# Linear attention with a two-layer network on one core: query features transposed by DMA, middle chunks in row halves

## The chip, the core and the metric

The kernel runs on one core of a Trainium2 chip. Its time is device microseconds of one execution. Five engines work at once, each through its own queue in order: TensorE (PE, with its weight loads as PEld), VectorE (DVE), ScalarE (ACT), GpSimd (POOL) and SyncE (SP), which issues all DMAs here. They wait for each other by semaphores.

## What is computed

For 8 batches x 8 heads, sequence 576, head size 64, 128 random features:

```python
def phi(x):                                   # x = q or k, scaled by 64 ** -0.25
    h = einsum('bhsd,md->bhsm', x, omega) - sum(x * x, -1) / 2
    return exp(h - max(h, -1)) / sqrt(m)
kv  = einsum('bhsm,bhsd->bhmd', phi(k), v)
num = einsum('bhsm,bhmd->bhsd', phi(q), kv)
den = einsum('bhsm,bhm->bhs', phi(q), sum(phi(k), 2))[..., None] + 1e-06
x   = (num / den)                             # to 4608 tokens x 512
h   = x @ w_in                                # 512 x 2048
out = (h * sigmoid(h)) @ w_out                # 2048 x 512
```

All of it is in fp32. The two large products of the network are done with operands cut into a high and a low part, three matmuls for one.

## The kernel before, in words

**Attention.** The 64 heads are taken as 32 pairs n = 0 to 31, four to a batch. A pair has 2 x 576 = 1152 rows, cut into nine chunks of 128; the fifth, the middle chunk (`MID`), has the last 64 rows of one head and the first 64 of the other. For the 24 pairs from the third batch on (`FOLD` holds the pairs of the first two), a pair's steps are these. Two projections (`project`, L477), one for k, one for q, make four chunks of each head; head size 64 fills only half the rows of the array, so that the two heads run in its two row halves at once. The middle chunks of k and q are two more products over the full height (`project_mids`, L495), on a tile with zeros in the unused half. Then maxima (`top`, `top_mids`), shifts, exponentials (`expo`, or `lower` and `expo_all`), the sums of k's features (`sums`, `zsum`), the denominators (`denom`), and q's features times their inverse (`normal`, on POOL, in three groups of three chunks). The features have rows along the partitions, and the last product needs them the other way. So each group of three chunks is transposed on TensorE into a PSUM bank (`turn`, L636) and copied to SBUF by ScalarE (`en_copy`, L640). The pair's last unit (`kv_numer`, "kvnum") multiplies them with kv, and makes kv of the next pair as well.

**The network.** Stages 1 and 2 (`stage1`, `stage2`), then blockwise products by Strassen's scheme in three levels (`deep`, `product`), all of them groups of three matmuls of 128x128 by 128x512 (`thrice`, L831). ScalarE and VectorE cut their operands into parts (L873, L877) and take the results out of PSUM. The attention units are let in between these products, and the products that need late tokens come late.

**The order.** Every step is a unit of a plan: engine, function, what it comes after, what tile of which ring it takes (`RINGS`) and what it frees. A written-out list (`RANK`) gives each unit its place; the units are issued in that order, so each engine's queue is in the order of ranks. `HOMES` says from which of three pools the units take their PSUM banks. `FILL` and `TRAIL` put extra matmuls on ones around named units, `warm` puts eight products on ones ahead of the first projection. The times in the plan's code are not used when the kernel runs.

Of the kernel before, what the change touches and what calls it, by code (L numbers as in the profile page):

```python
# [9 lines left out]
F32R = mybir.dt.float32r  # L10
U32 = mybir.dt.uint32
# [29 lines left out]
NORM_DVE = tuple(range(9, 12))  # L41
SQUARES = {}
# [5 lines left out]
FILL = {("turn", 3, 0): 4, ("turn", 3, 1): 1}  # L48
TRAIL = {("mid", 2, "q"): 9}
# [20 lines left out]
    "in": 4, "v": 2, "sq": 2, "hk": 2, "hq": 2,  # L70
    "mxk": 2, "mxq": 2, "nbk": 2, "nbq": 2, "mxm": 2, "nbm": 2, "t": 1, "es": 1, "kt": 1, "kw": 2,
    "en": 2, "den": 2, "rd": 2, "g0": 4, "g1": 4, "g2": 4, "g3": 4, "ts": 3, "w": 7, "ic": 2, "c": 3,
# [40 lines left out]
def turn_of(c):  # L113
# [8 lines left out]
    "mid": "full", "mids": "full", "z": "few",  # L122
# [17 lines left out]
class Plan:  # L140
# [225 lines left out]
def attention_mlp(ctx: ExitStack, tc: tile.TileContext, qX, kX, qS, kS, qT, kT, qn, kn, v, om_in, w_in, w_out, out):  # L366
# [52 lines left out]
    def load_raw(n, who):  # L419
# [5 lines left out]
        if n in FOLD:  # L425
            nc.sync.dma_start(both[:D, : 2 * S], (kS if who == "k" else qS)[b, k])
            return
        T["raw", n, who] = raw = both[:, : S + P]
        nc.sync.dma_start(raw, (kT if who == "k" else qT)[b - FOLDED, k])

    def load_nat(n, who):
# [1115 lines left out]
```

## Time and profile before

| | |
|---|---|
| median of 3 runs | 956.26 us (955.84 to 956.85) |
| profiled execution | span 954.4 us |
| TensorE busy | 942.7 us, 5740 matmul records |
| VectorE, ScalarE, POOL busy | 772.1, 619.8, 392.4 us |
| DMA | 237.87 MB, 73.0% of 16 engines' span |
| records of L831 (network) | 3120 |
| records of L636 (transposes of q's features) | 288 |

The page gives the span of the profiled execution; its whole time is not listed beside it, and the runs are 1.9 us longer than the span. Busy time of TensorE counts matmuls that overlap in its pipeline, so the starts of its records say more about pace than their lengths.

### The profile page before, as it was taken

The page shows a single profiled execution, that of the slowest core. Times are in us where ns is not written, and L with a number is a line of the kernel's source. Part 1 is how long each engine was busy: PE and PEld are TensorE (multiplying, and loading weights), DVE is VectorE, ACT ScalarE, POOL GpSimd, SP SyncE. Part 2 cuts the span into 40 slices and gives each one's busy share as a digit, 9 for nine tenths or more (in the row PEclk, how much of TensorE's full clock was granted, in tenths as well). Part 3 has the DMA queues.
Part 4 walks back from the last instruction along what each step waited for, and adds up shares of the span by engine and source line. Part 5 has one row for each costly group of instructions (what it writes and reads, how often), then busy time and mean ns, then how long its engine had stood idle before and what let it go on. Part 6 is the DMA issues. An engine that isn't in the chain of part 4 may idle for free.

```text
span 954.4 us, 16604 instructions
## 1 busy us (share of the span) xinstructions
PE 942.7 (99%) x5740; PEld 771.3 (81%) x5740; DVE 772.1 (81%) x1625; ACT 619.8 (65%) x1184; POOL 392.4 (41%) x430
## 2 busy tenths in 40 slices
PE   9999999999999999999999999999999999999998
PEld 8778888887888888777878888788888878888886
DVE  6899998698648988868988998879999774478964
ACT  7899886788787676897648866663547444225542
POOL 4676567786867676667323234222221000000000
PEclk9999999999999999999999999999999999999999
DMA  6379999989999798957758477646855566556662
GB/s 242 105 222 335 342 343 316 335 320 317 314 327 340 270 353 317 315 192 271 276 165 317 148 270 253 201 166 190 268 187 166 197 246 235 195 188 220 197 212 99
DMA packets 103219, 237.87 MB, mean 249 GB/s; under 512 B 13665, under 2 KB 44513, under 8 KB 103137
## 3 DMA queue, kind: packets, MB, share of 16 engines
q1 hardware_dynamic: 103136, 236.82, 73.0%
q8 instruction: 46, 0.75, 0.3%
q14 instruction: 37, 0.30, 0.1%
HBM read 192.74 MB, written 44.04 MB: 248 GB/s over the span
## 4 chain that ended last, share of the span: by engine, by line
PE 87%; DVE 6%; ACT 3%; DMA 2%; issue 1%; DVEq 0%; ACTq 0%; SPq 0%
PE ps_acc L831 58%; PE ps_h L831 11%; PE ps_att L477 2%; PE ps_att L595 2%; PE ps_h L477 1%; PE ps_att L657 1%; PE ps_h L636 1%; DVE prod L619 1%; PE ps_h L657 1%; PE ps_acc L477 1%; DMA in<-kX 1%; PE ps_h L595 1%; PE ps_acc L636 1%; PE ps_att L636 1%; DMA g<-w_in 1%
## 5 line engine op out<-in xcount | busy, mean ns | idle before, releaser
L831 PE MATMUL ps_acc<-ts,w 128*128 128x512 f32 x2544 | 600.7, 392 | 1.0 <-ACT hk L536 0.5
L831 PEld LDWEIGHTS ps_acc<-ts,w 128*128 128x128 f32 x2544 | 472.0, 188 | 99.0 <-ACT hk L536 0.7
L873 ACT CAST ts<-g 128x1024 fp32r<-128x1024 f32 x112 | 118.3, 1060 | 95.5 <-PE ps_acc L831 86.8
L877 DVE TENSOR_TENSOR ts<-g,ts 128x1024 fp32r<-128x1024 f32 x112 | 144.7, 1300 | 42.7 <-ACT ts L873 42.4
L831 PE MATMUL ps_h<-xq,w 128*128 128x512 f32 x576 | 142.2, 394 | 0.4 <-DVE xq L683 0.4
L831 PEld LDWEIGHTS ps_h<-xq,w 128*128 128x128 f32 x576 | 106.0, 188 | 22.1 <-DVE xq L683 0.9
L923 DVE TENSOR_TENSOR g<-ps_acc,g 128x512 f32<-128x512 f32 x144 | 93.5, 683 | 27.1 <-PE ps_acc L831 26.1
L630 POOL TENSOR_TENSOR hq<-hq,rd 128x384 f32<-128x384 f32 x87 | 81.8, 961 | 80.8 <-DVE rd L625 80.4
L565 POOL TENSOR_TENSOR t<-hk 128x256 f32<-128x256 f32 x64 | 54.8, 869 | 73.6 <-ACT hk L536 45.1
L869 DVE TENSOR_TENSOR g<-g,g 128x1024 f32<-128x1024 f32 x64 | 82.7, 1317 | 0.8 <-ACT g L927 0.6
L578 POOL TENSOR_TENSOR es<-t,es 128x256 fp32r<-128x256 f32 x32 | 27.7, 864 | 85.1 <-ACT es L574 74.0
L745 POOL TENSOR_TENSOR w<-g,w 128x512 fp32r<-128x512 f32 x32 | 46.7, 1474 | 30.7 <-ACT w L741 30.6
L889 ACT CAST ts<-xq 128x1024 fp32r<-128x1024 f32 x21 | 22.3, 1063 | 52.0 <-PE ps_acc L831 46.7
L619 DVE CUSTOM_DVE_ANT_0 prod<-hq,ps_att 128x128 f32<-128x128 f32 (+1 forms) x150 | 42.9, 286 | 10.4 <-PE ps_att L587 5.3
L927 ACT ACTIVATE g<-g 128x1024 f32<-128x1024 f32 x36 | 36.5, 1054 | 13.5 <-DVE g L923 13.4
L446 DVE TENSOR_REDUCE sq<-in 128x9 f32<-128x576 f32 x48 | 34.8, 739 | 11.1 <-ACT in L441 11.1
L570 POOL TENSOR_TENSOR t<-t,hk 64x128 f32<-64x128 f32 x64 | 35.9, 560 | 14.5 <-ACT hk L536 10.7
L950 DVE TENSOR_TENSOR c<-ps_acc,c 128x512 f32<-128x512 f32 x48 | 31.5, 682 | 10.4 <-PE ps_acc L831 10.4
L477 PE MATMUL ps_att<-oms,in 64*128 64x128 f32 x320 | 37.0, 279 | 0.2 <-ACT hk L536 0.2
L893 DVE TENSOR_TENSOR ts<-xq,ts 128x1024 fp32r<-128x1024 f32 x21 | 25.7, 1227 | 12.2 <-ACT ts L889 12.2
L477 PEld LDWEIGHTS ps_att<-oms,in 64*128 64x128 f32 x320 | 32.4, 187 | 3.7 <-issue 1.8
L619 DVE CUSTOM_DVE_ANT_0 prod<-hq,ps_acc 128x128 f32<-128x128 f32 (+1 forms) x100 | 28.6, 286 | 8.4 <-PE ps_acc L587 3.3
(212 smaller groups left out, 1548.3 us busy)
## 6 DMA issues: line engine op xcount, KB each, us to landing
w<-w_d SPq DMA_DIRECT2D x168, 512.0 KB, 4.8
w<-ws_d SPq DMA_DIRECT2D x48, 512.0 KB, 4.6
v<-v SPq DMA_DIRECT2D x32, 320.0 KB, 4.8
out<-c SPq DMA_DIRECT2D x17, 512.0 KB, 4.7
in<-kT SPq DMA_DIRECT2D x24, 352.0 KB, 4.6
in<-qT SPq DMA_DIRECT2D x24, 352.0 KB, 6.2
g<-w_in SPq DMA_DIRECT2D x16, 512.0 KB, 6.2
g<-w_out SPq DMA_DIRECT2D x16, 512.0 KB, 5.8
```

The source lines that it names most:

```text
L477: nc.tensor.matmul(ps[:, cols], T["raw", n, who][r, o : o + P], oms[r], start=True, stop=True)
L565: nc.gpsimd.tensor_tensor(t[:, i], e[:, 5 * i : 5 * i + 2], e[:, 5 * i + 2 : 5 * i + 4], ALU.add)
L570: nc.gpsimd.tensor_tensor(t[r, i - 3, 0], t[r, i - 3, 0], e[r, MID], ALU.add)
L619: nc.vector.tensor_tensor_reduce(out=prod[r], in0=e[r, c], in1=z[r, j * M : (j + 1) * M], scale=1.0, scalar=GUARD, op0=ALU.mult, op1=ALU.a ...
L630: nc.gpsimd.tensor_tensor(e[:, c], e[:, c], rd[:, c].unsqueeze(2).broadcast_to([P, 3, M]), ALU.mult)
L745: nc.gpsimd.tensor_tensor(lo, T["w", i], hi.bitcast(F32), ALU.subtract)
L831: nc.tensor.matmul(ps, w(a), x[:, b], start=first and n == 0, stop=last and n == 2, **more)
L869: nc.vector.tensor_tensor(out, a, b, ALU.subtract)
L873: nc.scalar.copy(g[:, 0], T["g", p, SOURCE[j], u])
L877: nc.vector.tensor_tensor(g[:, 1], T["g", p, SOURCE[j], u], g[:, 0].bitcast(F32), ALU.subtract)
L923: nc.vector.tensor_tensor(to, T["q", p, chain, i], T["g", p, r, i // 2][:, i % 2], ALU.add)
L927: nc.scalar.activation(g, g, AF.Silu)
```

## The change

- **Transposes.** For 15 pairs (`CROSS`: 13, 14, 15 and 20 to 31) the nine transposes on TensorE and the three copies go. ScalarE copies the features to two planes of 16-bit halves (`planes`), one DMA issued by SP transposes all 18 blocks of 128 x 128 (`cross`), and ScalarE puts the halves together (`words`).
- **Tiles.** The rings `hq` and `en` of two tiles each become one ring `f` of four, which also holds the planes and the transposed planes.
- **Middle chunks.** k's tile brings a tile in which k's and q's middle rows lie in the two row halves. Two half-height products run at once into two banks, so that each bank has 64 rows of k and 64 of q. Maximum, exponential and lowering take one instruction per bank or half.
- **Start.** Omega's load becomes a unit of SP's queue; by its rank it is issued after the first k tile. The fillers go, `warm` has a rank in the middle of the first pairs, and `first` lets the first product of a block come before the end of the block before it.
- **Order.** `RANK` (3681 units instead of 3726) and `HOMES` are new lists.

The lists, and the lines of the plan that only repeat costs and names, are left out here.

```diff
+CROSS = (13, 14, 15) + tuple(range(20, 32))
-FILL = {("turn", 3, 0): 4, ("turn", 3, 1): 1}
-TRAIL = {("mid", 2, "q"): 9}
+FILL = {}
+TRAIL = {}
-    "in": 4, "v": 2, "sq": 2, "hk": 2, "hq": 2,
+    "in": 4, "v": 2, "sq": 2, "hk": 2, "f": 4,
...
-        T["raw", n, who] = raw = both[:, : S + P]
+        T["raw", n, who] = raw = both[:, : S + P] if who == "k" else both[:, :S]
...
-    def project_mids(n, ps):
-        for i, who in enumerate("kq"):
-            nc.tensor.matmul(ps[:, i * M : (i + 1) * M], T["raw", n, who][:, S:], oms, start=True, stop=True)
-            T["p", n, who, 2] = ps[:, i * M : (i + 1) * M]
-        T["pm", n] = ps
-        T["h", n, "q"] = new("hq", [P, NC, M])
+    def project_mids(n, a, b):
+        for j, ps in enumerate((a, b)):
+            r = slice(j * D, (j + 1) * D)
+            nc.tensor.matmul(ps[:, :M], T["raw", n, "k"][r, S:], oms[r], start=True, stop=True)
+        T["pm", n] = a, b
+        T["h", n, "q"] = new("f", [P, NC, M])
...
-        nc.vector.tensor_reduce(T["mxm", n], T["pm", n][:, : 2 * M].rearrange("p (c m) -> p c m", m=M), AX.X, ALU.max)
+        for j, ps in enumerate(T["pm", n]):
+            nc.vector.tensor_reduce(T["mxm", n][:, 1 - j : 2 - j], ps[:, :M], AX.X, ALU.max)
...
+    def mid_sides(n, who):
+        for j, ps in enumerate(T["pm", n]):
+            i = j if who == "q" else 1 - j
+            r = slice(i * D, (i + 1) * D)
+            yield T["h", n, who][r, MID], ps[r, :M], T["nbm", n][r, 1 - j : 2 - j]
...
     def expo(n, who, j):
+        if j == 2 and n not in FOLD:
+            for to, ps, bias in mid_sides(n, who):
+                nc.scalar.activation(to, ps, AF.Exp, bias=bias)
+            return
...
     def lower(n, who, j):
+        if j == 2 and n not in FOLD:
+            for to, ps, low in mid_sides(n, who):
+                nc.vector.tensor_scalar(to, ps, low, None, ALU.add)
+            return
...
+    def planes(n):
+        T["pl", n] = to = flat(new("f", [P, NC, M])).bitcast(U16)
+        halves = flat(T["h", n, "q"]).bitcast(U16)
+        nc.scalar.copy(to.rearrange("p (b n) -> p b n", b=2), halves.rearrange("p (n b) -> p b n", b=2))
+
+    def cross(n):
+        T["tp", n] = to = flat(new("f", [P, NC, M])).bitcast(U16)
+        nc.sync.dma_start_transpose(out=to.rearrange("p (c t) -> p c t", t=P), in_=T.pop(("pl", n)))
+
+    def words(n):
+        T["en", n] = en = flat(new("f", [P, NC, P]))
+        halves = T.pop(("tp", n)).rearrange("p (b n) -> p b n", b=2)
+        nc.scalar.copy(en.bitcast(U16).rearrange("p (n b) -> p b n", b=2), halves)
...
-    add("load_omega", "ACT", 0.4, -9, load_omega, lat=0.1)
+    add("load_omega", "SP", 0.4, -9, load_omega, lat=0.1)
...
+            if n in CROSS:
+                continue
             add(("turn", n, g), "PE", 0.246, at(n, 9.5 + 0.1 * g, 44.2 + 0.8 * g), lambda ps, n=n, g=g: turn(n, g, ps),
...
+        if n in CROSS:
+            add(("pl", n), "ACT", 2.1, 0, lambda n=n: planes(n), after=[("norm", n, 2)], alloc=[("f", ("pl", n))], free=[("h", n, "q")])
+            add(("xp", n), "SP", 0.5, 0, lambda n=n: cross(n), after=[("pl", n)], alloc=[("f", ("tp", n))], free=[("pl", n)], lat=4.0)
+            add(("rc", n), "ACT", 2.1, 0, lambda n=n: words(n), after=[("xp", n)], alloc=[("f", ("en", n))], free=[("tp", n)])
...
-                order=[done] if done else [], alloc=[] if k else [("h", ("ph", t, f))],
+                order=[opened if k == 0 and t == 0 else done] if done else [], alloc=[] if k else [("h", ("ph", t, f))],
...
+    def both_mids(x, y):
+        x, y = (a.transpose(0, 1, 3, 2).reshape(-1, NPAIR, P, S) for a in (x, y))
+        top = np.concatenate([y[:, :, :D, MAIN:], x[:, :, :D, MAIN:]], axis=3)
+        low = np.concatenate([x[:, :, D:, :REST], y[:, :, D:, :REST]], axis=3)
+        return np.concatenate([x, np.concatenate([top, low], axis=2)], axis=3)
```

## Rows read from the trace of the kernel before

**Rows 1.** The page: busy time, share and instructions of each engine.

```profile
PE 942.7 (99%) x5740; PEld 771.3 (81%) x5740; DVE 772.1 (81%) x1625; ACT 619.8 (65%) x1184; POOL 392.4 (41%) x430
```

**Rows 2.** Windows: stretch, length, busy PE, PEld, DVE, ACT, POOL, clock, DMA, GB/s.

```profile
0.00:62.00 62.00, 57.15 (x598) 48.81 (x598) 48.99 (x161) 51.23 (x126) 35.56 (x54) 1.00 0.55 176
450.00:550.00 100.00, 99.91 (x616) 81.11 (x615) 92.06 (x191) 69.92 (x147) 32.65 (x38) 1.00 0.65 227
550.00:650.00 100.00, 100.00 (x658) 81.27 (x657) 86.88 (x193) 66.71 (x138) 30.24 (x35) 1.00 0.67 229
650.00:760.00 110.00, 110.00 (x606) 89.95 (x605) 98.63 (x207) 53.91 (x72) 22.21 (x30) 1.00 0.59 192
```

**Rows 3.** The chain of waits near its end: start, length, what.

```profile
771.68 156.62 PE ps_acc L831 x690
```

**Rows 4.** TensorE's timeline (start, length) around transposes and middle chunks.

```profile
565.65 8.44 PE L831 MATMUL ps_acc<-ts,w 128*128 128x512 f32 x36
573.93 0.49 PE L636 MATMUL ps_h<-ident,hq 128*128 128x128 f32 x3
...
574.83 1.63 PE L831 MATMUL ps_acc<-ts,w 128*128 128x512 f32 x6
576.30 0.61 PE L495 MATMUL ps_h<-oms,in 128*128 128x128 f32 x4
576.66 0.48 PE L587 MATMUL ps_acc<-es,ones 128*128 128x256 f32 x2
```

**Rows 5.** TensorE's timeline where a projection in row halves begins.

```profile
559.38 4.27 PE L831 MATMUL ps_acc<-ts,w 128*128 128x512 f32 x18
563.58 0.37 PE L477 MATMUL ps_acc<-oms,in 64*128 64x128 f32 x1
...
563.79 0.27 PE L477 MATMUL ps_acc<-oms,in 64*128 64x128 f32 x1
...
563.90 0.27 PE L477 MATMUL ps_acc<-oms,in 64*128 64x128 f32 x1
```

**Rows 6.** TensorE's warm-up and fillers by line; the chain's third k tile.

```profile
L400 PE MATMUL ps_att<-ones 128*128 128x128 f32 x16 | 3.6, 419 | 1.1 <-DVE ones L388 1.1
L415 PE MATMUL ps_h<-ones 128*128 128x128 f32 x20 | 2.7, 280 | 0.4 <-ACT hq L536 0.4
...
7.56 9.06 DMA in<-kX
```

**Rows 7.** ScalarE by line: busy us, mean ns, idle before.

```profile
L640 ACT COPY en<-ps_h 128x384 f32<-128x384 f32 x35 | 17.4, 498 | 4.3 <-PE ps_h L636 4.2
L557 ACT ACTIVATE hq<-hq 128x1152 f32<-128x1152 f32 x8 | 9.3, 1168 | 1.6 <-DVE hq L553 1.6
L536 ACT ACTIVATE hq<-ps_acc,nbm 128x128 f32<-128x128 f32 x5 | 2.0, 410 | 0.0
```

**Rows 8.** VectorE by line (one row from its timeline), then POOL.

```profile
L511 DVE TENSOR_REDUCE mxm<-ps_att 128x2 f32<-128x256 f32 x10 | 4.2, 418 | 2.4 <-PE ps_att L495 2.4
...
7.51 0.29 DVE L506 TENSOR_REDUCE nbk<-ps_h 128x1 f32<-128x128 f32 x1
...
L619 DVE CUSTOM_DVE_ANT_0 prod<-hq,ps_att 128x128 f32<-128x128 f32 (+1 forms) x150 | 42.9, 286 | 10.4 <-PE ps_att L587 5.3
...
L619 DVE DVE_READ_ACCUMULATOR2_ANT den<- 128x1 f32 (+1 forms) x320 | 25.9, 81 | 0.1
L630 POOL TENSOR_TENSOR hq<-hq,rd 128x384 f32<-128x384 f32 x87 | 81.8, 961 | 80.8 <-DVE rd L625 80.4
```

**Rows 9.** DMA issues, median us to landing; an issue on SP's timeline.

```profile
w<-w_d SPq DMA_DIRECT2D x168, 512.0 KB, 4.8
...
rest<-xr SPq DMA_DIRECT2D x32, 32.0 KB, 4.1
...
1.18 0.42 SPq L423 DMA_DIRECT2D in<-kX  x1
```

More of the change, by code (lines that the diff above doesn't have):

```diff
@@ L10 @@
 F32R = mybir.dt.float32r
+U16 = mybir.dt.uint16
 U32 = mybir.dt.uint32
@@ L121 @@
     "proj": "rows", "kv": "columns", "num": "columns", "kvnum": "columns", "turn": "turned", "ktt": "turned",
-    "mid": "full", "mids": "full", "z": "few",
+    "mid": "full", "mids": "rows", "z": "few",
 }
@@ L479, in project @@
         if n in FOLD or who == "k":
-            T["h", n, who] = new(f"h{who}", [P, NC, M])
+            T["h", n, who] = new("hk" if who == "k" else "f", [P, NC, M])
         if n not in FOLD:
@@ L524, in shift_mids @@
         shift_by(T["nbm", n], T["mxm", n], T["sq", n][:, :, 4])
-    def bias_of(n, who, c):
-        if c == MID and n not in FOLD:
-            i = "kq".index(who)
-            return T["nbm", n][:, i : i + 1]
-        return T["nb", n, who][:, c : c + 1]
+    def mid_sides(n, who):
[3 more added lines that the diff above has]
+            yield T["h", n, who][r, MID], ps[r, :M], T["nbm", n][r, 1 - j : 2 - j]
     def expo(n, who, j):
+        if j == 2 and n not in FOLD:
+            for to, ps, bias in mid_sides(n, who):
+                nc.scalar.activation(to, ps, AF.Exp, bias=bias)
+            return
         h, ps = T["h", n, who], T.pop(("p", n, who, j))
@@ L568, in sums @@
         else:
-            r = slice((i - 3) * D, (i - 2) * D)
+            a = i - 3 if n in FOLD else 4 - i
+            r = slice(a * D, (a + 1) * D)
             nc.gpsimd.tensor_tensor(t[r, i - 3, 0], t[r, i - 3, 0], e[r, MID], ALU.add)
@@ L630, in normal, with flat @@
         nc.gpsimd.tensor_tensor(e[:, c], e[:, c], rd[:, c].unsqueeze(2).broadcast_to([P, 3, M]), ALU.mult)
+    def flat(x):
+        return x.rearrange("p c m -> p (c m)")
+    def planes(n):
[9 more added lines that the diff above has]
+        nc.scalar.copy(en.bitcast(U16).rearrange("p (n b) -> p b n", b=2), halves)
     def turn(n, g, ps):
         if g == 0:
-            T["en", n] = new("en", [P, NC * P])
+            T["en", n] = flat(new("f", [P, NC, P]))
         for i in range(3):
@@ L1020, in attention_mlp @@
                     order=([("proj", n - 1, "k" if n - 1 in BOTH else who)] if n else []) + ([("mids", n)] if i and not fold else []),
-                    alloc=([(f"h{who}", ("h",) + w)] if fold or not i else []) + ([] if fold else [(f"mx{who}", ("mx",) + w)])
+                    alloc=([("f" if i else "hk", ("h",) + w)] if fold or not i else []) + ([] if fold else [(f"mx{who}", ("mx",) + w)])
                     + [(f"nb{who}", ("nb",) + w)], free=[])
@@ L1035, in attention_mlp @@
         if not fold:
-            add(("mids", n), "PE", 0.361, at(n, 2.9, 6.2 + 5.2), lambda ps, n=n: project_mids(n, ps), banks=1,
-                after=[("raw", n, "k"), ("raw", n, "q"), "omega2"], order=[("proj", n, "k")],
-                alloc=[("hq", ("h", n, "q")), ("mxm", ("mxm", n)), ("nbm", ("nbm", n))], free=[])
-            add(("topm", n), "DVE", 0.34, at(n, 3.5, 6.2 + 5.8), lambda n=n: top_mids(n), after=[("mids", n)])
+            add(("mids", n), "PE", 0.23, at(n, 2.9, 6.2 + 5.2), lambda a, b, n=n: project_mids(n, a, b), banks=2,
+                after=[("raw", n, "k"), "omega2"], order=[("proj", n, "k")],
+                alloc=[("f", ("h", n, "q")), ("mxm", ("mxm", n)), ("nbm", ("nbm", n))], free=[])
+            add(("topm", n), "DVE", 0.4, at(n, 3.5, 6.2 + 5.8), lambda n=n: top_mids(n), after=[("mids", n)])
             add(("nbm", n), "DVE", 0.28, at(n, 4, 6.2 + 6.0), lambda n=n: shift_mids(n), port=True,
@@ L1044, in attention_mlp @@
             plan.freed_by[("in", n, "k")] = [("mids", n), ("proj", n, "k"), ("ssum", n, "k")]
-            plan.freed_by[("in", n, "q")] = [("mids", n), ("proj", n, "k" if n in BOTH else "q"), ("ssum", n, "q")]
+            plan.freed_by[("in", n, "q")] = [("proj", n, "k" if n in BOTH else "q"), ("ssum", n, "q")]
         e = {}
@@ L1052, in attention_mlp @@
                 else:
-                    b = bk(("mids", n)) if j == 2 else bk(("proj", n, "k"), 2 * i + j) if n in BOTH else bk(("proj", n, who), j)
+                    b = None if j == 2 else bk(("proj", n, "k"), 2 * i + j) if n in BOTH else bk(("proj", n, who), j)
                     bias = [("nbm", n)] if j == 2 else [("nb", n, who)] + ([("mids", n)] if n in BOTH and i else [])
                 if direct:
-                    add(("exp", n, who, j), "ACT", 0.26 if j == 2 else 1.0,
+                    add(("exp", n, who, j), "ACT", (0.26 if fold else 0.5) if j == 2 else 1.0,
                         at(n, 3 * i + 2 + 0.1 * j, 6.2 + 6.2 + 0.1 * i if j == 2 else o + 1.6 + 0.1 * j),
-                        lambda n=n, who=who, j=j: expo(n, who, j), after=bias, table="exp", free=[b])
+                        lambda n=n, who=who, j=j: expo(n, who, j), after=bias, table="exp", free=[b] if b else [bk(("mids", n), x) for x in range(2)])
                 else:
-                    add(("low", n, who, j), "DVE", 0.26 if j == 2 else 0.61,
+                    add(("low", n, who, j), "DVE", (0.26 if fold else 0.52) if j == 2 else 0.61,
                         at(n, 3 * i + 2 + 0.1 * j, 6.2 + 6.2 + 0.1 * i if j == 2 else o + 1.5 + 0.1 * j),
-                        lambda n=n, who=who, j=j: lower(n, who, j), after=bias, free=[b])
+                        lambda n=n, who=who, j=j: lower(n, who, j), after=bias, free=[b] if b else [bk(("mids", n), x) for x in range(2)])
             if direct:
@@ L1111, in attention_mlp @@
                     after=[("den", n, 2)], order=[("norm", n, g - 1)] if g else [], free=[("rd", n)], port=True)
+            if n in CROSS:
+                continue
             add(("turn", n, g), "PE", 0.246, at(n, 9.5 + 0.1 * g, 44.2 + 0.8 * g), lambda ps, n=n, g=g: turn(n, g, ps),
-                after=[("norm", n, 0 if one else g)], order=[("turn", n, g - 1)] if g else ([("turn", n - 1, 2)] if n else []),
-                alloc=[] if g else [("en", ("en", n))], banks=1, free=[("h", n, "q")])
+                after=[("norm", n, 0 if one else g)], order=[("turn", n, g - 1)] if g else ([("turn", n - 1, 2)] if n and n - 1 not in CROSS else []),
+                alloc=[] if g else [("f", ("en", n))], banks=1, free=[("h", n, "q")])
             add(("en", n, g), "ACT", 0.37, at(n, 9.6 + 0.1 * g, 44.4 + 0.8 * g), lambda n=n, g=g: en_copy(n, g),
                 after=[("turn", n, g)], free=[bk(("turn", n, g))])
+        if n in CROSS:
+            add(("pl", n), "ACT", 2.1, 0, lambda n=n: planes(n), after=[("norm", n, 2)], alloc=[("f", ("pl", n))], free=[("h", n, "q")])
+            add(("xp", n), "SP", 0.5, 0, lambda n=n: cross(n), after=[("pl", n)], alloc=[("f", ("tp", n))], free=[("pl", n)], lat=4.0)
+            add(("rc", n), "ACT", 2.1, 0, lambda n=n: words(n), after=[("xp", n)], alloc=[("f", ("en", n))], free=[("tp", n)])
         t, k = divmod(n, NPAIR)
@@ L1120, in attention_mlp @@
         x_new = [("xq", ("x", t, k))] if t < ONCE else [] if k % 2 else [("xq", ("xb", t, k // 2))]
-        after = [("kw", n)] + [("en", n, g) for g in range(3)]
+        after = [("kw", n)] + ([("rc", n)] if n in CROSS else [("en", n, g) for g in range(3)])
         free = [("en", n), ("kw", n)]
@@ L1186, in attention_mlp @@
     pos = 0
-    done = prior = None
+    done = prior = opened = None
     loads, highs, lows = [], [], []
@@ L1195, in first @@
     def first(t, f):
-        nonlocal pos, done
+        nonlocal pos, done, opened
         if t:
@@ L1509, in padded, with crossed @@
         mixed = np.zeros((B, NPAIR, P, 2, D), a.dtype)
-        mixed[:, :, :D, 0] = a[:, :, :D, MID]
-        mixed[:, :, D:, 1] = a[:, :, D:, MID]
+        mixed[:FOLDED, :, :D, 0] = a[:FOLDED, :, :D, MID]
+        mixed[:FOLDED, :, D:, 1] = a[:FOLDED, :, D:, MID]
+        mixed[FOLDED:, :, D:, 0] = a[FOLDED:, :, :D, MID]
+        mixed[FOLDED:, :, :D, 1] = a[FOLDED:, :, D:, MID]
         return np.concatenate([a[:, :, :, :MID], mixed, a[:, :, :, MID + 1 :]], axis=3)
+    def crossed(k, q):
+        k, q = rows(k), rows(q)
+        x, y = k[FOLDED:, :, :, MID].copy(), q[FOLDED:, :, :, MID].copy()
+        k[FOLDED:, :, :D, MID], k[FOLDED:, :, D:, MID] = x[:, :, D:], y[:, :, D:]
+        q[FOLDED:, :, D:, MID] = x[:, :, :D]
+        return {"kn": k, "qn": q}
     def stack(a):
@@ L1522 @@
         "kS": stack(k[:FOLDED]),
-        "qT": cols(q[FOLDED:]),
-        "kT": cols(k[FOLDED:]),
-        "qn": rows(q),
-        "kn": rows(k),
+        "qT": np.ascontiguousarray(q[FOLDED:].transpose(0, 1, 3, 2)).reshape(-1, NPAIR, P, S),
+        "kT": both_mids(k[FOLDED:], q[FOLDED:]),
+        **crossed(k, q),
         "v": padded(rows(v)),
```

18 lines of the change are left out of this document (8 added, 10 removed), and 371 rows, old and new, of the table RANK.

## Prediction

> **What bounds the kernel now.** I read the page's busy line first, then the windows by stage, TensorE's timeline around the attention work, then ScalarE, VectorE and the DMA rows. The page says that TensorE is busy for 942.7 of 954.4 us [rows 1]. Busy matmuls overlap, so this alone does not prove a bound. The chain of waits does: near its end it is one run of 690 matmuls of L831 in 156.62 us [rows 3], which is 0.227 us per matmul, and this pace returns wherever a long run stands. The program has 3120 such matmuls: 708 us that the change does not touch. The rest of the span is attention work, let in between them, and a short list of real idling. The windows show where: TensorE idles 4.85 us in the first 62 us, and from 450 to 760 us next to nothing (0.09 us of 310) [rows 2]. So after 62 us a microsecond taken from TensorE's queue is a microsecond of the span, as long as nobody else is late. The reader is to see who could be: VectorE is busy 92% of 450 to 550 us, 87% and 90% of the next two stretches, ScalarE 70% and less [rows 2].
>
> **Time base.** The profiled span is 954.4 us. The median of the runs is 956.26, so 1.9 us lie around the span; I keep them. A difference under 0.2% (1.9 us) I call none.
>
> **Transposes taken from TensorE.** A pair's nine transposes come in three groups of three. Around 574 us all nine stand alone between big matmuls: 36 of these start at 565.65, so at 0.227 each they are over at 573.82; the transposes start at 573.93, and the next big matmul at 574.83 [rows 4]. All nine and the two switches cost 1.01 us. A group by itself costs no less per piece. Fifteen pairs: 15 x 1.01 = 15.2 us off TensorE.
>
> **The middle chunks.** Before, k's and q's middle chunks are two full-height products, one after the other: six big matmuls from 574.83 are over at 576.19, the middle chunks start at 576.30 and what follows at 576.66 [rows 4]: 0.47 us, 24 times, 11.3 us. After, they are two half-height products at once. A pair of half-height products runs in two steps: in the projection the steps on the two bank halves start at 563.58, 563.79 and 563.90, so 0.21 us for the first and 0.11 for each later one; the big run before it (18 from 559.38) ends at 563.47, so entering costs 0.11 [rows 5]. Sorted by rank, 16 of the 24 new middle chunks touch a projection, which is in the same shape already: two steps, 0.22 us. The other eight pay for entering and leaving as well: 0.11 + 0.21 + 0.11 + some 0.12 = 0.55. Sum 16 x 0.22 + 8 x 0.55 = 7.9 us: 3.4 us less. I take 2.5, since a few of the old ones shared their switch with a transpose that goes away as well.
>
> **The new order on TensorE.** Big runs are broken by attention work at 95 places instead of 107, but nine transposes or turns of kv now stand directly ahead of kv's column-shaped products. I leave this at zero, give or take 1 us. The sum for TensorE is 15.2 + 2.5 = 17.7 us less.
>
> **The start.** The 14 filler matmuls go (28 records; 20 of them are 2.7 us [rows 6]) and the 16 warm-up records (3.6 us) move from ahead of the first projection to behind a transpose of pair 2. Omega's load moves from the first to the second place on SP's queue, one issue later. In this stretch TensorE waits for others: the load of k's third tile is on the chain for 9.06 us [rows 6], VectorE is busy 49 of 62 us and ScalarE 51 [rows 2], so the fillers' end shortens nothing for certain. The warm-up's records take 419 ns, the fillers' of the same form, later, 280 [rows 6]: the engine began at its lower level, 1.2 GHz, and had the upper one after that work. Now the first two projections, some 4 us at full clock, would begin low and lose up to 4 us. The wait for k's third tile covers it, since of four 512 KB weight loads queued ahead of that tile three are left. If that cover is gone, it costs 2 to 4 us. I take 0, with -3 to +4.
>
> **ScalarE.** Two 2304-element copies per pair are new (two-byte halves apart, and together again). A copy of 384 elements takes 498 ns and a pass over 1152 takes 1168 [rows 7]: 0.87 ns an element more, so 2.17 us each, 30 of them: 65.1 us. Going: 45 of the 384-element copies, 22.4 us. The middle chunks' exponentials double in 16 pairs: 32 more at 0.41 us, 13.1 us. Net +56 us, 620 to 676 us, 72% of the new span; in 450 to 760 us from 61% to about 77%. No bound.
>
> **VectorE.** The maximum of the middle chunks is two instructions of 0.29 us for one of 0.417: +0.16 us x 24 = 3.9 us; in eight pairs the lowering doubles, 16 x some 0.3 = 5 us [rows 8]. It sets nothing in the mean (781 of 938 us); see the second rival.
>
> **SP and the transposing DMA, the open price.** Each of 15 pairs adds one issue on SP (0.42 us for a load of k [rows 9]) that waits for ScalarE's copy, with the loads of weights queued behind it; they are issued several products ahead, so a wait of some microseconds reaches nobody. It moves 590 KB within SBUF. No row shows a transposing DMA. From below: it lands like a 512 KB weight load, 4.8 us after issue (rows of the DMA list; a gain over TensorE's path is excluded, since the copies come on top). From above: as 18 blocks of 128 x 128 that wait for each other, each as long as a 32 KB store, 4.1 us [rows 9]: 74 us. I take 6 us, near the lower end, because it is a single instruction of the size of the weight load and its bytes cross the same 16 engines, which have room (65% and 67% busy from 450 to 650 us [rows 2]).
>
> What is late next: the pair's last product waits for the copy together (2.17 us) behind the DMA. I sorted the new lists and took, for each pair, the work that TensorE still has between the matmul that lets SP get past the load ahead of the transpose, and the product that needs it. The tightest are pairs 31 (eight products of six matmuls, 48 x 0.227 = 10.9 us), 21 (11.1), 26 (11.5), 22 (12.3), 27 (14.0), 25 (16.5) and 29 (19.1); the rest have 20 to 40. Two issues, the copy together and handoffs need 3.5 us of that. So a landing of up to 7.4 us is hidden everywhere, and at 6 us, with some loads ahead in the queue, I charge 2 us in all. ScalarE works in order, so a late landing also holds the casts behind the copy; they have a few products of lead. The other path into it runs from the pair's sums (z). It is shortest in pair 21, 18.1 us: ten denominators at 286 and 81 ns, three multiplications at 961 on POOL [rows 8], 2.17, 0.42, 6 and 2.17, which is 17.3 us without handoffs, so it just fits.
>
> By the Trainium skill, DMA: Bandwidth & Descriptors, section Latency and other measured facts, a transposing DMA moves 261 GB/s: 590 KB would take an estimated 2.3 us on top of the fixed part, which is the hidden case. VectorE: DVE Perf Modes of the same skill, section The three transpose paths, speaks against the change: it gives 1309 ns for one 128 x 128 block on the crossbar against 390 ns on TensorE, and advises TensorE where PSUM will do; 18 blocks in series would be an estimated 23.6 us, the first rival. No run here shows either yet.
>
> **Sum.** 956.3 - 15.2 - 2.5 + 0 + 2 = 940.6; I forecast 940 us.
>
> **Rival 1, the transposes are slow (other side).** The 18 blocks go one after another. For it: the trace has no row that excludes it, and the 32 KB rows show that small pieces land hardly sooner than big ones. Against it: one instruction. At a landing of 11.7 us (18 issues of 0.42 us, then 4.1 us), 15.2 us are needed, and pairs 31, 21, 26, 22 and 27 are late by 4.3, 4.1, 3.7, 2.9 and 1.2 us: 16 us, time 956, no change. It decides at about 12 us: each further microsecond then costs five to eleven. At 20 us the lateness sums to 75 us: 1015 us.
>
> **Rival 2, VectorE takes over.** From 450 to 760 us it is busy 277.6 of 310 us [rows 2]. TensorE's work there falls by 12 pairs' transposes and 11 middle chunks, 13 us; VectorE's grows by 4. With 282 of 297 us, in order, and with casts of ScalarE to wait for, it may keep the stretch as long as it was. Then only what is saved outside counts: about 5 to 9 us, time 949. Against it: the lists can put attention's VectorE work later, where it is less busy (pair 31's last product moves from 2340 to 2454 big matmuls).
>
> **Rival 3, better than the sum.** The new start saves some microseconds beside the rest: 933.
>
> **Chances.** Forecast (936 to 946) 0.55; rival 2 (946 to 953) 0.15; rival 1 near its deciding point (953 to 962) 0.08, beyond it 0.16; rival 3 0.06. Range: 934 to 962 takes in the forecast, rival 2 and the mild end of rival 1, with a part of rival 3: 0.80. The forecast's own range is 936 to 946. Faster 0.76, same 0.06, slower 0.18.
>
> **What would show it.** Right: transposes on TensorE fall from 288 to 153 records; the windows from 450 us on still show TensorE full but the stages end some 15 us sooner; transposing DMAs land within 8 us; the copies take 2.1 us; middle chunks behind a projection cost 0.22 us. Wrong: TensorE's idle rows at the kv products, released by ScalarE's copy together; SP busy for long in the transpose's issue; idle ahead of L831 released by VectorE from 450 to 760 us; a granted clock under 1.00 behind the start.

## The result, and the profile after

Four runs after the change have a median of 943.99 us (943.35 to 945.32), against 956.56 us for the kernel before, run beside them. The ratio is 0.9866, 95% interval 0.9851 to 0.9881: 12.6 us, or 1.3%, faster. The prediction was 940 us, a gain of 16.3; the gain is 3.7 us short of that, and the time lies inside the forecast's own range (936 to 946). The profiled execution has a span of 943.2 us, 11.2 less than before. It is the longest of the four runs (945.32), so the trace shows about 1.3 us less gain than the median. Where runs of a kernel fell into a slower state of the chip, only its fast runs are compared; below this concerns one kernel, the old order with ScalarE as issuer, whose two fast runs are given and whose trace is of a slow one.

The page's busy line, which answers to [rows 1]:

```profile
PE 925.8 (98%) x5577; PEld 749.6 (79%) x5577; DVE 757.6 (80%) x1665; ACT 683.3 (72%) x1201; POOL 383.3 (41%) x430
```

The windows by stage, with the columns of [rows 2]:

```profile
0.00:62.00 62.00, 54.01 (x566) 46.06 (x567) 48.74 (x161) 52.37 (x125) 38.94 (x56) 1.00 0.69 216
62.00:250.00 188.00, 186.75 (x1179) 151.29 (x1178) 156.94 (x403) 148.31 (x293) 132.38 (x141) 1.00 0.93 317
250.00:450.00 200.00, 197.29 (x1228) 157.45 (x1227) 151.01 (x363) 168.53 (x339) 130.76 (x134) 1.00 0.89 307
450.00:550.00 100.00, 98.52 (x596) 79.01 (x595) 92.97 (x194) 86.50 (x154) 28.00 (x36) 1.00 0.77 246
550.00:650.00 100.00, 99.98 (x648) 79.69 (x648) 89.23 (x225) 85.63 (x142) 32.57 (x41) 1.00 0.80 262
650.00:760.00 110.00, 110.00 (x582) 89.22 (x579) 98.03 (x172) 68.51 (x71) 16.43 (x22) 1.00 0.69 219
```

Busy TensorE fell by 16.9 us (942.7 to 925.8), and the span by only 11.2: the rest is 5.7 us more idling, 3.1 of it in the first 62 us (7.99 against 4.85) and 1.4 from 450 to 760 us (1.50 against 0.09). VectorE is as busy as before where the second rival feared for it. ScalarE is what filled up: from 450 to 650 us it went from 70 and 67 to 87 and 86 us per 100.

TensorE's waits (what, for whom, us in total, times, longest) say who is late now:

```profile
PE ps_h L467 <- ACT omr L405: 4.8, 1, 4.8
PE ps_att L593 <- ACT hk L535: 1.2, 1, 1.2
PE ps_acc L601 <- ACT f L535: 1.0, 1, 1.0
PE ps_att L488 <- ACT f L540: 0.8, 1, 0.8
```

The first is the start: without a warm-up in front, TensorE idles until omega is scaled. All of the view's rows sum to 13.0 us, 10.7 released by ScalarE; before it was 7.6 and 4.2. The next ones are exponentials (L535, L540), not the new copy. That ScalarE reaches them later because it has more to do fits its fuller windows; no run takes it apart. No row of the whole view has the copy together (L653) as its releaser.

The new route's own rows, first ScalarE's two copies on the page (busy us, mean ns, idle before), then the transposing DMA by its line:

```profile
L653 ACT COPY f<-f 128x2304 uint16<-128x2304 uint16 x15 | 42.4, 2827 | 4.9 <-DMA f<-f 4.8
L644 ACT COPY f<-f 128x2304 uint16<-128x2304 uint16 x15 | 31.7, 2114 | 7.6 <-POOL f L636 7.5
```

```profile
L648 SPq DMA_TRANSPOSE f<-f x15: 1809/2792/7170, 301.5 to 775.5; - x15
...
  ACT f L653: 4.8, 3
DMA to landing us min/median/max: 3.9/4.9/10.8
```

Three of 15 landings made ScalarE wait, 4.8 us in all. The landing takes 4.9 us in the median, near the low end of the predicted bounds. What nothing before had shown is the first row: SP is held by the issue for 1.8 to 7.2 us, not for 0.42 [rows 9].

**A balance by starts.** For the text below I gave every group of TensorE's queue the distance from its start to the next group's that is usual for its shape and its neighbour's, called work, and what goes beyond it wait. Counted from the k projection of pair 6 on (at 65.22 us before, 66.03 after), work falls from 877.8 to 861.6 us and wait grows from 6.2 to 10.2. So -16.1 + 4.1, and +0.8 for the start: the 11.2 us of the trace. What is usual is a choice. With each distance set against the median of its shape and the next one's in all traces, the same count gives -16.9 and +4.8; for the runs below it gives 16.7 where the text has 15.65, 14.7 for 15.0, 3.5 for 4.4 and 3.0 for 2.9. A term is good to about 1 us.

### The profile page after: what moved, and what is told of

Same layout as the page of the kernel before. It is cut to its first block, busy times and chain, and to the rows that moved or that the text cites. A ratio compares the mean times of both kernels' runs of the same rounds, so it can differ in the third digit from the quotient of the medians.

```text
span 943.2 us, 16380 instructions
## 1 busy us (share of the span) xinstructions
PE 925.8 (98%) x5577; PEld 749.6 (79%) x5577; DVE 757.6 (80%) x1665; ACT 683.3 (72%) x1201; POOL 383.3 (41%) x430
## 4 chain that ended last, share of the span: by engine, by line
PE 83%; DVE 4%; ACT 4%; DMA 4%; POOL 2%; issue 1%; SPq 1%; DVEq 0%; POOLq 0%; ACTq 0%
PE ps_acc L854 56%; PE ps_h L854 11%; DMA w<-w_d 2%; PE ps_h L476 2%; PE ps_acc L476 2%; PE ps_att L601 1%; DMA ws_d<-ic 1%; PE ps_att L476 1%; PE ps_att L680 1%; PE ps_acc L601 1%; PE ps_h L467 1%; PE ps_h L601 1%; PE ps_h L680 1%; DVE prod L625 1%; POOL ic L826 1%
## 5 line engine op out<-in xcount | busy, mean ns | idle before, releaser
L896 ACT CAST ts<-g 128x1024 fp32r<-128x1024 f32 x112 | 117.1, 1055 | 68.4 <-PE ps_acc L854 57.4
L900 DVE TENSOR_TENSOR ts<-g,ts 128x1024 fp32r<-128x1024 f32 x112 | 138.6, 1252 | 34.3 <-ACT ts L896 33.9
L636 POOL TENSOR_TENSOR f<-f,rd 128x384 f32<-128x384 f32 x87 | 80.4, 947 | 63.0 <-DVE rd L631 45.2
L570 POOL TENSOR_TENSOR t<-hk 128x256 f32<-128x256 f32 x64 | 49.9, 791 | 119.9 <-ACT hk L540 71.1
L892 DVE TENSOR_TENSOR g<-g,g 128x1024 f32<-128x1024 f32 x64 | 80.4, 1266 | 4.7 <-ACT g L887 4.2
L768 POOL TENSOR_TENSOR w<-g,w 128x512 fp32r<-128x512 f32 x32 | 44.8, 1409 | 32.6 <-ACT w L764 29.0
L625 DVE CUSTOM_DVE_ANT_0 prod<-f,ps_att 128x128 f32<-128x128 f32 (+1 forms) x150 | 42.9, 286 | 11.2 <-PE ps_att L593 2.7
L653 ACT COPY f<-f 128x2304 uint16<-128x2304 uint16 x15 | 42.4, 2827 | 4.9 <-DMA f<-f 4.8
L644 ACT COPY f<-f 128x2304 uint16<-128x2304 uint16 x15 | 31.7, 2114 | 7.6 <-POOL f L636 7.5
L476 PE MATMUL ps_h<-oms,in 64*128 64x128 f32 x264 | 34.4, 280 | 0.4 <-ACT f L535 0.4
```

Of the source, the lines that this page charges most:

```text
L476: nc.tensor.matmul(ps[:, cols], T["raw", n, who][r, o : o + P], oms[r], start=True, stop=True)
L570: nc.gpsimd.tensor_tensor(t[:, i], e[:, 5 * i : 5 * i + 2], e[:, 5 * i + 2 : 5 * i + 4], ALU.add)
L625: nc.vector.tensor_tensor_reduce(out=prod[r], in0=e[r, c], in1=z[r, j * M : (j + 1) * M], scale=1.0, scalar=GUARD, op0=ALU.mult, op1=ALU.a ...
L636: nc.gpsimd.tensor_tensor(e[:, c], e[:, c], rd[:, c].unsqueeze(2).broadcast_to([P, 3, M]), ALU.mult)
L653: nc.scalar.copy(en.bitcast(U16).rearrange("p (n b) -> p b n", b=2), halves)
L768: nc.gpsimd.tensor_tensor(lo, T["w", i], hi.bitcast(F32), ALU.subtract)
```

## The experiments

Twelve kernels, each timed beside the kernel before. Ratios are to that kernel; the changed kernel has 0.9866.

### Is the gain TensorE's own time?

```diff
+            for g in range(3):
+                add(("dum", n, g), "PE", 0.33, 0, again_turn, banks=1, free=[bk(("dum", n, g))])
```

> The changed kernel, unchanged but for 135 transposes more on TensorE, of a constant into a free bank and read by nobody: nine for each of the 15 pairs, three ahead of each of the last three blocks before the product with kv. No other engine's work, no wait and no place in a queue changes. Theory (the change's gain is TensorE's own time, at 15 x 1.01 us): 943.9 + 15.2 = 959 us, 957.5 to 960. Rival (part of it falls into waits that TensorE has there anyway, 3.6 us of them released by ScalarE between 62 and 760 us more than the kernel before has): 954 to 957 us.

969.9 us, ratio 1.0127 (1.0103 to 1.0151): 26 us more, where the theory had 15.2, so its range fails. The balance separates two parts. Work is 15.65 us more, the theory's price. The other 10.9 us are waits, and the dummy transposes' own rows hold most of them:

```profile
PE ps_att L679 <- ACT hk L555: 2.5, 1, 2.5
PE ps_h L679 <- DVE hk L573: 2.5, 1, 2.5
PE ps_h L679 <- ACT g L906: 2.3, 1, 2.3
PE ps_h L679 <- ACT f L550: 1.7, 1, 1.7
```

L679 is the dummy transpose. Nobody reads it, but it needs a PSUM bank, and waits 9.0 us in all for others to empty one. So in these places a transpose on TensorE costs its time and the wait for a bank.

```diff
-CROSS = (13, 14, 15) + tuple(range(20, 32))
+CROSS = ()
```

> The changed kernel with its order kept, but with q's features of all 32 pairs transposed on TensorE again (just ahead of each pair's product with kv), and no copies into planes, transposing DMAs and copies back into words. Theory (the saving is TensorE's own time): 135 transposes come back at 15 x 1.01 = 15.2 us, so about 959 us, 1.016 of the changed kernel. Rival (the gain comes from the order searched anew): under 950 us. Second rival (the copies and the crossbar route cost new waits that now vanish, some 2.4 us of them): about 956.5 us.

987.42 us, ratio 1.0317 (1.03 to 1.0334). Work is 15.0 us more than in the changed kernel, again the predicted term. The remaining 28 us are waits at the transposes and what follows from them: where I put them, three of a pair share banks that ScalarE's small copies empty only behind other work. So this run confirms the term, not the total, and says nothing of how well this order could do with better places for them. How much a new order alone would give the kernel before is not tested.

### The middle chunks

```diff
-    def project_mids(n, a, b):
-        for j, ps in enumerate((a, b)):
-            r = slice(j * D, (j + 1) * D)
-            nc.tensor.matmul(ps[:, :M], T["raw", n, "k"][r, S:], oms[r], start=True, stop=True)
+    def project_mids(n, ps):
+        for i, who in enumerate("kq"):
+            nc.tensor.matmul(ps[:, i * M : (i + 1) * M], T["raw", n, who][:, S:], oms, start=True, stop=True)
```

> The changed kernel with the middle chunks of the 24 pairs from 8 on as two full-height products one after the other, as before, in one bank instead of two; order kept but for two loads that move by some 20 places. Theory: 24 x (0.33 - 0.22) = 2.6 us come back on TensorE and nothing else: 946.6 us, 946 to 947.5. Rival (the half-height matmuls cost VectorE and ScalarE as much by doubling their small instructions as they save TensorE): 943 to 944.5 us.

954.19 us, ratio 0.9966 (0.9953 to 0.9979), some 10 us more than the changed kernel. To see whether the moved loads did it:

> The full-height middle chunks in the changed kernel again, with other small moves to make room for q's raw tile: the middle chunk of pair 23 goes 12 places earlier and one load of pair 27 some 20 places later, the load of pair 25 stays where it was. In the first such run TensorE's own work was 4.4 us more (not 2.6), and 5.3 us of its 8.0 us of added span stood in one place, behind a transposing DMA of pair 22 that landed 9.4 us after its issue and a ScalarE that waited 4.9 us for it. Theory (that jam came from the moved load and is no part of the mids' price): no such jam, 946.6 to 948.5 us. Rival (the longer middle chunks themselves push the route of pair 22 late): 951 us or more again, with the jam.

952.63 us, ratio 0.995 (0.9936 to 0.9964), and the jam is there again (it belongs to pair 24's transposing DMA; the expectation's "pair 22" was a misreading). Its rows on SP's and ScalarE's timelines (start, length):

```profile
561.13 0.33 SPq L718 DMA_DIRECT2D rest<-xr  x1
562.54 5.73 SPq L656 DMA_TRANSPOSE f<-f  x1
568.31 1.05 SPq L858 DMA_DIRECT2D w<-w_d  x2
```

```profile
571.94 2.76 ACT L661 COPY f<-f 128x2304 uint16<-128x2304 uint16 x1 [5.21 <-DMA f<-f]
574.57 1.98 ACT L904 CAST ts<-g 128x1024 fp32r<-128x1024 f32 x2
```

and the same step of the changed kernel on SP's timeline:

```profile
555.86 0.49 SPq L710 DMA_DIRECT2D rest<-xr  x1
561.85 1.84 SPq L648 DMA_TRANSPOSE f<-f  x1
```

There SP had issued its last load 5.5 us earlier, here 1.1 us earlier; the issue held SP 5.73 instead of 1.84 us, and the piece landed 9.4 us after its start. ScalarE stood in front of its copy for 5.21 us, with the casts (L904) of TensorE's next operands behind it. The theory that the moved load was to blame fell; whether the longer chunks or my remaining moves set it off stays open. TensorE's own work is 4.4 us more in both runs by this balance (3.5 by the other), not 2.6. That the half-height form also saves switches of shape in the new order would explain the rest, but is not shown.

### The start

```diff
-    202, 2, 3, 6, 0, ...
+    0, 3, 4, 7, 1, ...      # RANK: "warm" first, the rest as it was
```

> The changed kernel with the eight warm-up products put in front again; TensorE idles until 4.8 us otherwise, and its first projections run at the low clock (0.21 us instead of 0.11 between matmuls until about 9 us). Theory (the missing warm-up costs the start 1 to 3 us): about 942 us, 941 to 943. Rival (the start is set by the loads and VectorE's and ScalarE's work on the first four pairs, so TensorE's clock there is hidden): 943.5 to 944.5 us, no change.

943.45 us, ratio 0.9859 (0.9841 to 0.9876): no difference that can be told. In the changed kernel the first projections do run slowly; these are its first rows on TensorE's timeline and one from when the pace has changed:

```profile
4.82 0.58 PE L467 MATMUL ps_h<-omr,in 64*128 64x128 f32 x1 [4.82 <-ACT omr L405]
...
8.40 0.42 PE L467 MATMUL ps_h<-omr,in 64*128 64x128 f32 x1
...
10.57 0.27 PE L467 MATMUL ps_h<-omr,in 64*128 64x128 f32 x1
```

0.42 against 0.27 us are the two lengths that warm-up and fillers had [rows 6]; the granted clock of the windows reads 1.00 here and does not show it. But pair 6's k projection starts at 65.55 instead of 66.03 us, no more: with the warm-up first, TensorE waits 2.4 us for ScalarE's copy kt at 42 us (0.6 us without it). And the granted clock reads 0.57 from 44 to 48 us, right behind this wait: near the lower of its two levels (1.2 GHz of 2.4), where the changed kernel has 1.00. TensorE's row and the window (columns as before):

```profile
44.20 0.42 PE L621 MATMUL ps_acc<-ident,kt 128*128 128x128 f32 x1 [2.42 <-ACT kt L618]
44.00:48.00 4.00, 3.80 (x20) 3.81 (x20) 3.96 (x11) 3.65 (x8) 2.38 (x3) 0.57 0.75 223
```

So what TensorE gains at the start it gives back, to ScalarE and to the lower clock. That VectorE holds the stage up as well, as the rival had it, is not shown.

### The transposing DMA

```diff
-        nc.sync.dma_start_transpose(out=to.rearrange("p (c t) -> p c t", t=P), in_=T.pop(("pl", n)))
+        nc.sync.dma_start(to, T.pop(("pl", n)))
```

> The changed kernel with each of the 15 transposing DMAs replaced by a plain copy of the same tile (same bytes, same source and target), so q's features of these pairs enter the products untransposed. Theory (the transposing form holds SP's queue 2.8 us a piece in the trace, and the loads behind it come late: the 1.1 us wait at 339 us and parts of others): 942 to 943 us, SP's hold under 0.6 us. Rival (nobody waits for what stands behind it on SP's queue): 943.5 to 944.5 us.

943.84 us, ratio 0.9864 (0.9849 to 0.988): the rival. The line of the DMA:

```profile
L648 SPq DMA_DIRECT2D f<-f x15: 470/487/512, 302.7 to 775.6; - x15
...
DMA to landing us min/median/max: 3.0/4.1/7.9
```

In the median SP is free 2.3 us sooner and the piece lands 0.8 us sooner; neither is worth anything in this order.

```diff
+        pl = T.pop(("pl", n))
+        for _ in range(2):
+            nc.sync.dma_start_transpose(out=to.rearrange("p (c t) -> p c t", t=P), in_=pl)
```

> The changed kernel with each transposing DMA issued twice, the second behind the first, so a landing takes about twice as long (about 10.5 us in place of 4.9); nothing else changes. Prediction's table of distances: up to 7.4 us is hidden everywhere and 11.7 us costs 16, so about +11 us, 955. By the changed kernel's own trace, from the planes' end to the copy back's start and from that copy's end to the product: pairs 15, 21, 25, 26, 29 and 31 would be late by 3.0, 4.4, 3.0, 2.7, 3.2 and 3.6 us, +20 us, 964. Rival (the landing isn't tight anywhere, ScalarE sets when the copies run): under 947 us.

993.78 us, ratio 1.0398 (1.0375 to 1.0422): 50 us more, and both tables are far too low. They had counted how late the products with kv would be, and the largest losses are elsewhere. ScalarE waits for landings 36.0 us (11 times, 4.8 before) with everything behind it; TensorE waits for loads that stood behind SP, of which there was nearly nothing before:

```profile
PE ps_acc L601 <- DMA v<-v: 5.6, 2, 2.9
PE ps_acc L856 <- DMA w<-w_d: 4.3, 2, 3.3
PE ps_h L856 <- DMA w<-w_d: 2.6, 1, 2.6
PE ps_acc L856 <- DMA w<-ws_d: 2.5, 2, 2.0
```

```diff
-        nc.sync.dma_start_transpose(...)
+        nc.scalar.dma_start_transpose(...)
```

> The changed kernel, unchanged but for the engine that issues the transposing DMAs: ScalarE in place of SP. In the changed kernel's trace SP waits 69 us in all, up to 9.6 us at once, ahead of these 15 issues, with weights behind it. Theory (those waits no longer hurt, as the order was laid out around them, and ScalarE pays some 15 x 2.5 us more): 944 to 950 us, waits of TensorE for ScalarE up. Rival (SP's waits still cost the 1.1 us at 339 us and parts of others): 941.5 to 943 us.

1035.45 us, ratio 1.0824 (1.0806 to 1.0842). Both theories were wrong by 90 us. From ScalarE's queue the same DMA lands far later, and that engine waits for it:

```profile
L648 ACTq DMA_TRANSPOSE f<-f x15: 1769/4144/10330, 296.8 to 861.3; - x15
...
DMA to landing us min/median/max: 4.1/8.2/23.7
```

```profile
ACT f L653 <- DMA f<-f: 65.0, 9, 22.2
```

```profile
PE ps_acc L854 <- ACT ts L896: 27.7, 4, 19.3
PE ps_acc L854 <- ACT f L535: 8.0, 1, 8.0
PE ps_att L680 <- ACT f L653: 7.9, 1, 7.9
```

ScalarE is held by the issue itself for 4.1 us in the median, and a landing of up to 23.7 us stops it in front of the copy together, with the casts (L896) behind. Loads on SP's queue, no longer held back there, may fill the DMA engines at that moment. The trace goes with it: the two slowest landings (18.4 and 23.7 us) had six loads each issued while the issue held ScalarE, the two quickest (4.1 and 4.2 us) none, and from SP's queue there were none in any of the 15. No run shows that this is the cause. By the Trainium skill, DMA: Bandwidth & Descriptors, section Issuing engines are not separate DMA queues, all DMAs share the 16 engines whoever starts them, and another issuer saves only the usually small time of the issue. For this DMA the runs differ: the issue is long on either engine, and the median landing went from 4.9 to 8.2 us.

### The order

```diff
 # kernel before, its own RANK and HOMES, plus CROSS, planes, cross, words; the ring f
+        if n in CROSS:
+            add(("pl", n), "ACT", ...); add(("xp", n), "SP", ...); add(("rc", n), "ACT", ...)
```

> The kernel before, in its own order and with its middle chunks, warm-up and loads, with one part of the change alone: the 15 pairs' features go by two ScalarE copies and a transposing DMA (planes and DMA right behind the normalisation, the copy back two blocks ahead of the product with kv). In the trace of before the time from the end of the normalisation to that product is 8.2, 9.0 and 9.1 us for pairs 13, 15 and 21 and 11 us or more for the other twelve; the new route takes 2.1 + 5.4 + 2.8 + 0.5 = 10.8 us. Theory (TensorE's 15.2 us are saved and the three tight pairs give back 2.6 + 1.8 + 1.7 = 6.1): 956.6 - 15.2 + 6.1 = 947.5 us, 945 to 950. Rival (a ScalarE that waits in order for landings holds up the rest, so the route needs the order made for it): 954 us or more. Second rival (the order adds nothing): 941 to 943 us, the mids' 2.5 us apart from the changed kernel.

1023.68 us, ratio 1.0702 (1.0689 to 1.0716): the rival, and worse than it said. TensorE's waits name the loads:

```profile
PE ps_acc L859 <- DMA w<-w_d: 21.3, 4, 12.7
PE ps_h L859 <- DMA w<-w_d: 10.2, 1, 10.2
PE ps_att L606 <- DMA v<-v: 4.7, 1, 4.7
```

39.2 of the view's 63.8 us are released by a DMA. The transposing DMA itself lands in 3.9 us here, quicker than in the changed kernel. What is slow is SP: it waited 168 us in all ahead of these 15 issues (the expectation's 157 was added up wrongly), 146 of it released by ScalarE, up to 18.3 us at once (69 and 9.6 in the changed kernel), and the weights stood behind. The waits have a second price: the mean granted clock is 0.969. It is 0.92 from 250 to 450 us, where TensorE idles for 21 us, and 0.91 from 550 to 650, where it idles for 12 (1.00 before in both):

```profile
250.00:450.00 200.00, 178.86 (x985) 144.09 (x984) 135.45 (x285) 133.31 (x253) 114.83 (x115) 0.92 0.79 269
```

In this run 63 of the network's matmuls follow each other at 0.427 us and not at 0.227, in the trace of before none. The mean clock is below 1.00 in the other runs with long waits too (0.991 with the transposes back, 0.985 with each DMA issued twice, 0.965 with ScalarE as issuer), so a part of their time is this price. Two runs were to tell whether SP is all of it.

```diff
 # units in the order of RANK, as around pair 24
 norm 24, pl 24
-xp 24
 exp 26, ..., raw 27 k, raw 27 q, ..., nat 27 k, ..., pr (1, 3, 4)
-rc 24
 pr (1, 3, 5), ..., w2 (1, 6, 1), w2 (1, 6, 2)
+xp 24, rc 24
 w2 (1, 6, 3), ..., kvnum 24
```

> The old order with the crossbar route again (1024 us in the first try, where each transposing DMA stood on SP's queue right behind the planes' copy), with only the places of the 45 new instructions moved: each transposing DMA goes behind the loads that SP issued, in the trace of before, until the planes are ready, and each copy back behind the block that TensorE reached when the piece would have landed. Theory (the 67 us over the kernel before came from SP: it runs ahead of the other engines, met each transposing DMA early, waited for the copy, some 157 us in all, and held the weights behind it): late products cost 7.7 us by before's trace (pairs 13, 15, 21 and 29), two DMAs must still stand 8 to 10 us too early (pairs 13 and 30), so 956.9 - 15.2 + 7.7 + 0 to 8 = 949 to 957 us. Rival (ScalarE's copies, waiting in order, are what the old order can't hold): 980 us or more.

```diff
-        nc.sync.dma_start_transpose(...)      # in the first try, nothing else changed
+        nc.scalar.dma_start_transpose(...)
```

> The first try in the old order (1024 us), unchanged but for the engine that issues the 15 transposing DMAs: ScalarE, right behind its own copy into planes, in place of SP. Theory (SP's waits held the weights): the waits of TensorE for weights (34.5 us) and v (4.7 us) go, with what followed from them; the late products (6.1 us) stay, and ScalarE pays for 15 issues of 2 to 3 us: 948 to 960 us. Rival (ScalarE waiting in order holds up the rest): 985 us or more, with TensorE waiting for ScalarE's casts and exponentials.

1015.8 us, ratio 1.0608 (1.0582 to 1.0633), and, with ScalarE as issuer, 1057.48 and 1071.96 us, ratio 1.1128 (1.1067 to 1.1189). The theory fell in both. Its first half is right: with better places on SP, TensorE's waits released by DMAs go from 39.2 to 18.8 us, and without these DMAs on SP's queue to 1.3. But those released by ScalarE go from 17.1 to 27.0, and to 100.3. In the run with better places on SP, ScalarE now waits for landings 13 times:

```profile
ACT f L658 <- DMA f<-f: 33.4, 13, 4.3
```

So two in-order queues must suit the route at once, and easing one moved waits to the other.

```diff
-CROSS = (13, 14, 15) + tuple(range(20, 32))
+CROSS = (12, 13, 14, 15, 16, 17) + tuple(range(20, 32))
```

> The changed kernel with pairs 12, 16 and 17 on the crossbar route too (18 pairs in all), the rest of the order kept. In the changed kernel's trace the normalisation ends 14.8, 7.3 and 8.9 us ahead of these pairs' products with kv; the route takes 10.8 us. Theory (TensorE saves 3.0 us; pair 12 fits, pair 16 gives back 3.5 and pair 17 1.9 us of waits, with more behind them on ScalarE, which is 84% busy there): 946 us or more. Rival (TensorE's time is all that counts): 941 us.

973.05 us, ratio 1.0165 (1.0152 to 1.0178). Work falls by 2.9 us, as both theories had it, and the waits grow by 32. The largest are again weights, at the places of pairs 12 and 17, where SP did nothing for 11.8 and 21.8 us ahead of the transposing DMA's issue:

```profile
PE ps_h L865 <- DMA w<-w_d: 10.5, 1, 10.5
PE ps_acc L865 <- DMA w<-w_d: 9.4, 1, 9.4
```

I had put the DMA right behind the planes' copy, and SP met it early. That 10.8 us between normalisation and product are enough is refuted: pair 12 had 14.8 and cost over 10.

## Why the prediction was right, and where it was short

Against the sum of 940.6 us, a gain of 15.7, the trace's 11.2 lacks 1.6 us of TensorE's work (16.1 of 17.7), 2.1 in new waits (4.1 for 2) and 0.8 at the start.

**TensorE as the bound.** Right in its price. The two runs that gave it the transposes back raised its work by 15.0 and 15.65 us; the predicted term was 15.2. Their totals rose by 43 and 26 us, so that what shows the term is the balance, not the time. The 153 records of transposes (L659) are as predicted.

**The middle chunks and the order on TensorE.** Predicted -2.5 and 0; together they came to about -1.1 (16.1 less 15.0; -0.2 to -2.2 by the other count). Behind a projection they cost the predicted 0.22 us:

```profile
558.67 1.06 PE L476 MATMUL ps_att<-oms,in 64*128 64x128 f32 x16
559.57 0.27 PE L495 MATMUL ps_h<-oms,in 64*128 64x128 f32 x1
...
559.68 0.27 PE L495 MATMUL ps_h<-oms,in 64*128 64x128 f32 x1
```

The second step starts 0.11 us behind the first and takes as long. Taken back in the new order, the chunks are worth 4.4 us, or 3.5; so the order's switches cost some 1 to 3 us by these balances, at or beyond the end of the 1 us either way that I had allowed. TensorE's sum is the first part that was mis-sized; how its 1.6 us divide between chunks and order is not settled.

**The start.** Taken as 0, measured +0.8, and moving the warm-up gives nothing: the cover held, though what I can show is a wait for ScalarE and a fall of the clock behind it, and not the third k tile.

**The new waits.** Taken as 2 us, measured 4.1. This is the second part of the shortfall. The prediction looked for them at the kv products; in the trace they sit at exponentials and copies of ScalarE, the engine that got fuller. ScalarE came out at 683 us, not 676, mostly as the copy together takes 2.83 us and not 2.17; the copy into planes (2.11) was right. 72% of the span seemed no bound, but the engine is 86% full where the pairs are.

**The open price.** 6 us was taken and 4.9 measured. The piece costs no more than 0.8 us over a plain copy of its size. The Trainium skill, DMA: Bandwidth & Descriptors, section Latency and other measured facts, had led to an estimated 2.3 us beside the fixed part; the shortest landing, 3.9 us, leaves 1.6 for the fixed part, which no run shows by itself. The 23.6 us estimated from the Trainium skill, VectorE: DVE Perf Modes, section The three transpose paths, no landing on SP's queue came near (11.3 us at most). 13 of 15 landings are within the 8 us that I had named. What I had wrong is the issue, 2.8 us and not 0.42. An SP that is busy for long in the issue stood among the signs of being wrong, and it came; the run with a plain copy shows that it costs nothing here. That is luck as far as the working goes: it is owed to an order in which nobody waits for what stands behind.

**Rival 1** was right in its form and its deciding point too late. It put 12 us of landing at no gain and each further microsecond at 5 to 11. Issued twice, which takes some 8.5 us (4.6 from the first issue to the second, by the median of their starts, and 3.9 to land), the change is already 37 us slower than before. The table of distances counted one product for each pair, and not the two queues behind it. The run holds SP for two issues as well, so it does not price a late landing alone.

**Rival 2** did not happen: VectorE is 89 to 93% busy from 450 to 760 us and TensorE idles 1.5 us there.

**What the prediction didn't see.** It took the new order as a neutral part of the change. In the places that I tried, the route loses without it: the old order with the route is 67 us slower than without it, and 59 in the better of the two further tries. My theories of a single wait that makes it so fell one after the other. What the runs do show is that SP's queue and ScalarE's queue both carry it; which order would suit both with full-height chunks or with more pairs was not found.

None of the twelve beats the changed kernel by more than can be measured.

## What to carry to other kernels

Moving work off the bound engine is worth that engine's time for it, and the balance by starts measures it to about a microsecond in kernels whose totals are 50 us apart; but the total is set by what the new steps stop in the queues they join. A DMA that waits for a computation belongs behind the loads that the issuing engine can issue meanwhile, and an engine that waits for its landing should have nothing urgent behind it: here each place had to be searched for both at once. Judge such a change only with its order, and an order only with the work it was made for.

## What the hardware showed that I had not expected

The issue of a transposing DMA holds SP longer when other DMAs are under way. In the changed kernel it took 1.81 to 2.45 us for the five with at most two DMAs issued in the 8 us before, and 2.55 to 7.17 for nine of the ten with three or more (the tenth, 1.84, had its last load end 5.5 us before). Over the nine traces that have it on SP, a better guide is how many DMAs were issued but not landed when it started: with none, 57 of 60 issues took 1.75 to 2.5 us and the longest 3.6; with four or more, all 24 took 2.78 to 7.7. The landing comes 1.9 to 2.2 us after the issue's end in 12 of the changed kernel's 15, so a long issue is a late landing. A plain DMA of the same tile takes 0.47 to 0.51 whatever precedes it. The reason is not shown. From ScalarE's queue the landing spread from 4.1 to 23.7 us, from SP's from 3.9 to 10.8, with the same tiles. A 16-bit copy of 2304 elements on ScalarE takes 2.11 us when it writes whole planes and reads every second half-word, and 2.83 us the other way round.
